# Attention on one Trainium2 core: an own order of two steps for the first half of the rows

## The chip, the cores and the metric

The kernel runs on one core of a Trainium2 chip. The metric is the device time of one execution in microseconds (us); lower is better. Before the change it is 2920.76 us, the median of three runs (2920.69 to 2922.99).

## What is computed

A transformer block for one sequence of 2048 rows and 576 columns, float32: a modulation drawn from a condition vector, layer norm, softmax attention with 32 heads of 18 columns, a second layer norm, and a gated product with 4608 hidden columns. The attention is what matters here:

```python
q, k, v = qkv[0], qkv[1], qkv[2]
scale = Dh ** -0.5
scores = jnp.einsum("bhqd,bhkd->bhqk", q, k) * scale
p = _softmax(scores, axis=-1)
o = jnp.einsum("bhqk,bhkd->bhqd", p, v)
```

## The kernel before

The attention is cut into 32 **units** `u`: units 0 to 15 are the first 1024 query rows, one unit for each pair of heads, and units 16 to 31 the other 1024 rows. A unit has 16 **steps** `kt`, one for each tile of 128 keys. Two steps in a row, an even and an odd one, are called a pair of steps here, so a unit has eight. TensorE's instructions run in the order in which the program writes them (lines 922 and 923 fix that); the order of the other engines is made by the framework's planner, from what is ready.

What a step issues is spelled by a string, one letter for each act (line 47: one string for even steps, one for odd steps):

- **t** (line 959): the transposed scores of 128 keys by 512 queries, one matmul of 56 rows. There are four in a step, for two chunks of queries and the two heads. The heads alternate, t0 and t2 take head 0, t1 and t3 head 1. Head 0 lies on partitions 0 to 63, head 1 on 64 to 127. ScalarE turns the result into `p` with an exponential (line 963).
- **m** (`turn`, line 490): one more piece of `maxima` (lines 426 to 469), which runs 64 pieces a unit, about one and a half units ahead: a score matmul of 54 rows (line 446), again with the heads alternating, of which VectorE takes the maximum of each row (line 459). From the third unit's maxima on, of every eight pieces the first goes to a relu on ScalarE (line 452), and the third is then taken by a VectorE operation (line 454) that adds the relu's result; the six others are plain maxima. In the first two units' maxima all eight are plain.
- **v** (`values`, line 528): the products of the oldest step's `p` with the values, four matmuls on four column strips of 32, which the trace shows as eight. A run of these is a **value run**. They add up in the one bank `o` over the 16 steps.
- **w** (lines 551 and 553): in odd steps, side work. `taken` (line 546) copies the finished `o` to `oT` on ScalarE, in the step kt = 1; `outputs` (line 554) transposes `oT` by four matmuls and scales it, at kt = 3; `spread` (line 471) transposes the maxima of the next unit, and its DMAs write them into the unit's `q` tile, at kt = 13. From unit 15 on, w also takes pieces of the projection behind the attention.

Every score matmul and every transpose takes the next of seven PSUM banks in turn (`bank`, line 78), so each waits until the work on the bank seven places before it is done. `p` has three buffers (line 520).

The two strings before are, with the acts numbered as above:

```python
STEPS = "vtmmttmvtm", "tmttwmtmm"
```

An even step holds two value runs, for the two steps before it, and an odd step none. Between the two runs lie t0, m, m, t1, t2, m; behind the second, t3, m, and then the odd step's t0, m, t1, t2, w, m, t3, m, m. `turns["to"]` caps how far `maxima` may be ahead; 89 pieces are done before the loop starts, and each step then does four.

Of the kernel before, what the change touches and what calls it, by code (L numbers as in the profile page):

```python
# [27 lines left out]
H = 32  # L28
DH = 18
VW = DH + 1  # L30
NT = S // P
# [7 lines left out]
LEAD = 6  # L39
# [4 lines left out]
NB = F // 256  # L44
LAG = 2

STEPS = "vtmmttmvtm", "tmttwmtmm"
ORDERED = 56


# [1 line left out]
def tile_block(ctx, tc, x_in, wqkv, wo, w_gate, w_up, w_down, c_in, w_mod, out):  # L52
# [20 lines left out]
    small = left.enter_context(tc.tile_pool(name="small", bufs=2))  # L73
    sc = early.tile([P, 5], F32, name="sc")

    turns = {"s": 0, "to": 65 + 4 * LEAD, "bank": 0}

    def bank():

        turns["bank"] += 1  # L80
        return ps.tile([P, 512], F32, name=f"s{turns['bank'] % 7}")


    def load_mod(a, b, i):

        cols = slice(2 * D * i, 2 * D * (i + 1))
        for t in range(0, 4, 2):
            rows = slice(t * P, (t + 2) * P)
            nc.sync.dma_start(a[:, t : t + 2, :], w_mod[rows, cols].rearrange("(t p) c -> p t c", p=P))
        nc.sync.dma_start(b[0:64, :], w_mod[DM:D, cols])  # L90
        return [a[:, t, :] for t in range(4)] + [b]
# [311 lines left out]
    def heads(u):  # L403
        return qsets[u % 3], ksets[u if u < 2 else 2 + (u - 2) % 3]

    def load_heads(u):


        qs, ks = heads(u)
        half, p = divmod(u, H // 2)  # L410
        own = slice(half * HW, (half + 1) * HW)
        for h in range(2):
            rows = slice((2 * p + h) * DH, (2 * p + h + 1) * DH)
            two, one = (slice(64 * h + a, 64 * h + b) for a, b in ((0, 2 * DH), (2 * DH, 3 * DH)))
            nc.sync.dma_start(
                qs[two, :].bitcast(F32), qd[:, rows, own].rearrange("l f n -> f l n").bitcast(F32)
            )
            nc.sync.dma_start(qs[one, :].bitcast(F32), qd[0, rows, own].bitcast(F32))
            wide = S if h or u < 2 else S + 512
            nc.sync.dma_start(  # L420
                ks[two, 0:wide].bitcast(F32),
                kd[0, rows, 0:wide].unsqueeze(1).to_broadcast([DH, 2, wide]).bitcast(F32),
            )
            nc.sync.dma_start(ks[one, 0:wide].bitcast(F32), kd[1, rows, 0:wide].bitcast(F32))
# [65 lines left out]
    def turn():  # L490
        if turns["s"] < turns["to"]:
            turns["s"] += 1
            next(todo, None)
# [52 lines left out]
    def taken():  # L546

        if "whole" in state:
            half, p, acc = state.pop("whole")
            oT = epool.tile([P, 512], F32, name="oT")  # L550
            nc.scalar.copy(oT, acc)  # L551
            state["end"] = (half, p, oT)

    def outputs():

        if "end" not in state:
            return
        half, p, oT = state.pop("end")
        tp = bank().rearrange("p (b q) -> p b q", q=P)
        for b in range(4):  # L560
            nc.tensor.transpose(tp[:, b, :], oT[:, b * P : (b + 1) * P], ident)  # L561

        tq = tp.rearrange("p b (j e) -> p j b e", e=32)
        rec = epool.tile([P, 4, 4], F32, name="rec")
        nc.vector.reciprocal(rec, tq[:, :, :, DH])
        if half == 1 and p == H // 2 - 1:
            state["last"] = epool.tile([P, 512], F32, name="oT")[:, 0 : 16 * DH].rearrange("p (t e) -> p t e", t=8)
            for h in range(2):
                nc.vector.tensor_tensor(
                    state["last"][:, :, h * DH : (h + 1) * DH].rearrange("p (c b) e -> p c b e", c=2),  # L570
                    tq[:, 2 * h : 2 * h + 2, :, 0:DH],
                    rec[:, 2 * h : 2 * h + 2, :].unsqueeze(3).to_broadcast([P, 2, 4, DH]),
                    op=ALU.mult,
                )
            return
        nc.scalar.copy(oT, tp.rearrange("p b q -> p (b q)"))
        tq = oT.rearrange("p (b j e) -> p j b e", j=4, e=32)
        for h in range(2):
            f0 = (2 * p + h) * DH
            nc.gpsimd.tensor_tensor(  # L580
                Os[half][:, :, f0 : f0 + DH].rearrange("p (c b) e -> p c b e", c=2),
                tq[:, 2 * h : 2 * h + 2, :, 0:DH],
                rec[:, 2 * h : 2 * h + 2, :].unsqueeze(3).to_broadcast([P, 2, 4, DH]),
                op=ALU.mult,
            )
# [341 lines left out]
    for u in range(UNITS):  # L927
        half, p = divmod(u, H // 2)
        qs, ks = heads(u)
        if 0 < u < UNITS - 2:  # L930
            load_heads(u + 2)
        if u == H // 2:
            Os.append(big.tile([P, 8, 640], F32, name="big"))
        for kt in range(NT):
            step = u * NT + kt
            turns["to"] = 65 + 4 * LEAD + 4 * (step + 1)
            kcols = slice(kt * P, (kt + 1) * P)
            probs = []
            for does in STEPS[kt % 2]:
                if does == "m":  # L940
                    turn()
                elif does == "w":
                    if kt == 3:
                        outputs()
                    taken()
                    if "spread" in state:
                        spread(*state.pop("spread"))
                    if FROM0 <= step < FROM1:
                        next(rows0, None)
                    if step >= FROM1:  # L950
                        next(rows1, None)
                elif does == "v":
                    if step >= LAG:
                        values()
                else:
                    c, h = divmod(len(probs), 2)
                    sT = bank()
                    rows = slice(64 * h, 64 * h + 3 * DH + 2)
                    nc.tensor.matmul(  # L959
                        sT, ks[rows, kcols], qs[rows, c * 512 : (c + 1) * 512], start=True, stop=True  # L960
                    )
                    pr = ppool.tile([P, 512], F32, name=f"p{len(probs)}")
                    state["exp"] = nc.scalar.activation(pr, sT, AF.Exp, scale=SCALE)  # L963
                    probs.append(pr)
            pending.append((half, p, kt, probs))
            if u in (1, 3):
                if kt == 2:
                    a = big.tile([P, 8, 640], F32, name="big")
                    a = a.rearrange("p a b -> p (a b)")[:, 0 : 8 * D].rearrange("p (t c) -> p t c", t=4)
                    b = slots.tile([P, 2560], F32, name="w0")[:, 0 : 2 * D]  # L970
                    mods = load_mod(a, b, 1 + u // 2)
                    row = slots.tile([P, 2560], F32, name="w1")[:, 0:544]
                elif kt == 10 and u == 1:
                    modulate(row, mods, HALVES, [(None, None), (mcol2[:, 1, :], 0.0)])
                elif kt == 10:
                    modulate(row, mods, HALVES, [(mcol2[:, 0, :], 1.0), (gb_b, None)])
            if 4 * NT <= step < FROM0 and step % 2 == 0:
                next(downs, None)
            if step == FROM0:
                for _ in downs:  # L980
                    pass
            if step == FROM1 - 1:
                for _ in rows0:
                    pass
                bgs.close()
                raws = ctx.enter_context(tc.tile_pool(name="raws", bufs=1, side="right"))
            if u == 30 and kt == 7:
                first = [load_block(raws, 0, k, paced) for k in range(2)]
            if u >= 30 and kt == 2:
                load_x(u - 30, f"k{u - 30}")  # L990
            if u == UNITS - 1 and kt == 3:
                nc.sync.dma_start(oend[:, :, 0 : D - DL - 2 * DH], Os[1][:, :, DL : D - 2 * DH])
            if u == UNITS - 1 and kt == 9:
                for _ in rows1:
                    pass
                load_x(2, "w0")
                load_x(3, "w1")
                both = big.tile([P, 2, 5, 512], F32R, name="big")
                for i in range(2):
                    X[5 + i] = both[:, i]  # L1000
                    load_x(5 + i)
                begun = {"b": 0, "half": 0, "raw": first}
                for k in ORDER[:2]:
                    weights_operand(begun, k, True)
# [196 lines left out]
    for n, (hf, b, k) in enumerate(seq):  # L1201
# [51 lines left out]
        if hf == 0 and b == NB - 1:  # L1253
            s = ORDER.index(k)
# [31 lines left out]
```

## Time and profile before

| | |
|---|---|
| median of three runs | 2920.76 us |
| the profiled execution | 2920.71 us |
| its span, first to last instruction | 2918.9 us |
| TensorE's granted clock over the span | 0.993 of full |
| busy share of PE / DVE / ACT / POOL | 98% / 73% / 55% / 28% |
| units 0 to 15 (237.5 to 896.9 us) | 659.4 us |
| units 16 to 31 (896.9 to 1588.8 us) | 691.9 us |
| the gated product (1588.8 us to the end) | 1330.1 us |

The profile's page gives busy time by engine; the windows give it by stage. A busy PE says little by itself: a matmul's record lasts longer than the interval at which the next one starts. So the stage is read by the start times of matmuls, from one value run to the next, and by what each of them waited for.

### The profile page before, as it was taken

How to read it: one execution, taken by the hardware profiler on the slowest of the kernel's cores; microseconds unless marked ns; L12 is line 12 of the kernel's file. 1: busy time of each engine (PE TensorE's matmuls, PEld its weight loads, DVE VectorE, ACT ScalarE, POOL GpSimd, SP SyncE). 2: the span in 40 equal slices, each digit the busy share in tenths (PEclk: the TensorE clock that was granted, in tenths of full speed). 3: DMA queues.
4: the chain of work that ended last, by engine and by line, in shares of the span. 5: the costliest groups of instructions: out<-in, count | busy, mean ns of one | idle time of the engine just before them, and what ended most of it. 6: DMA issues, size and time to landing. Idle time of an engine off the chain costs nothing.

```text
span 2918.9 us, 46640 instructions
## 1 busy us (share of the span) xinstructions
PE 2855.8 (98%) x17141; PEld 1880.8 (64%) x17141; DVE 2135.0 (73%) x3896; ACT 1614.4 (55%) x3022; POOL 814.1 (28%) x972
## 2 busy tenths in 40 slices
PE   7999999999999999999999999988999999999999
PEld 5874333343334443443443888877888888888888
DVE  7567888888888888998882777756777555555555
ACT  3227889999998888999888333333333111111111
POOL 3102014444213111661103544467543100000000
PEclk9999999999999999999999999999999999999999
DMA  5344123333212110221125866676666844444443
GB/s 176 115 147 145 49 76 131 122 125 123 90 49 77 34 53 21 99 95 63 50 86 185 289 220 234 232 250 237 225 211 238 300 167 169 167 168 167 159 159 137
DMA packets 137261, 425.97 MB, mean 146 GB/s; under 512 B 18884, under 2 KB 56520, under 8 KB 124744
## 3 DMA queue, kind: packets, MB, share of 16 engines
q1 hardware_dynamic: 121272, 342.42, 34.7%
q0 software_dynamic: 15760, 80.56, 7.8%
q8 instruction: 135, 2.21, 0.3%
q14 instruction: 94, 0.77, 0.1%
HBM read 264.45 MB, written 157.95 MB: 145 GB/s over the span
## 4 chain that ended last, share of the span: by engine, by line
PE 89%; DMA 3%; ACT 3%; DVE 2%; POOL 2%; issue 1%; SPq 1%; POOLq 0%; ACTq 0%; DVEq 0%
PE o L537 17%; PE x L1031 14%; PE d L1067 14%; PE s L959 13%; PE s L446 11%; PE bg L1031 5%; PE bu L1031 5%; PE s L294 3%; PE s L334 2%; PE s L676 2%; ACT p L963 2%; DMA xs<-ho 1%; DMA B<-hs 1%; PE s L561 1%; ACT oT L551 1%
## 5 line engine op out<-in xcount | busy, mean ns | idle before, releaser
L963 ACT ACTIVATE p<-s 128x512 f32<-128x512 f32 x2048 | 1068.5, 608 | 141.2 <-PE s L446 91.8
L459 DVE TENSOR_REDUCE mx<-s 128x1 f32<-128x512 f32 x1568 | 1015.4, 685 | 142.2 <-PE s L446 128.2
L446 PE MATMUL s<-k,q 54*128 54x512 f32 x1920 | 649.2, 439 | 2.1 <-ACT p L963 1.6
L959 PE MATMUL s<-q,k 56*128 56x512 f32 x1920 | 578.5, 433 | 2.7
L959 PEld LDWEIGHTS s<-q,k 56*128 56x128 f32 x1920 | 274.5, 185 | 472.2 <-ACT p L963 304.0
L537 PE MATMUL o<-p,vaug 128*32 128x512 f32 x4096 | 555.0, 607 | 0.0
L1067 PE MATMUL d<-wd,hh 128*128 128x288 f32 x2304 | 469.4, 298 | 20.9 <-DVE Oa L1071 20.7
L1067 PEld LDWEIGHTS d<-wd,hh 128*128 128x128 f32 x2304 | 379.0, 191 | 29.9 <-DVE Oa L1071 24.4
L1071 DVE TENSOR_TENSOR Oa<-Oa,d 128x288 f32<-128x288 f32 x576 | 257.8, 452 | 151.4 <-PE d L1067 147.8
L446 PEld LDWEIGHTS s<-k,q 54*128 54x128 f32 x1920 | 308.1, 185 | 69.2 <-ACT p L963 38.5
L1067 PE MATMUL d<-wd,hl 128*128 128x288 f32 x1152 | 343.7, 298 | 0.1
L1031 PE MATMUL x<-k,w 128*128 128x512 f32 x994 | 238.3, 390 | 0.5 <-DVE u L1245 0.5
L1043 ACT ACTIVATE u<-u 128x512 f32<-128x512 f32 x72 | 45.5, 632 | 328.9 <-DVE u L1233 310.3
L1067 PEld LDWEIGHTS d<-wd,hl 128*128 128x128 f32 x1152 | 219.7, 191 | 0.3 <-DVE hl L1047 0.3
L1031 PEld LDWEIGHTS x<-k,w 128*128 128x128 f32 x994 | 184.1, 188 | 37.5 <-DVE u L1245 0.9
L537 PEld LDWEIGHTS o<-p,vaug 128*32 128x32 f32 x4096 | 83.5, 108 | 164.7 <-issue 149.2
L1040 ACT ACTIVATE sg<-x 128x512 f32<-128x512 f32 x36 | 21.5, 598 | 285.1 <-PE x L1031 285.1
L1073 POOL DMA_DIRECT2D out_dram<-Oa x16 | 8.7, 544 | 606.4 <-DVE Oa L1071 606.4
L454 DVE CUSTOM_DVE_ANT_0 rise<-s,rise 128x512 f32<-128x512 f32 x240 | 163.4, 681 | 0.0
L452 ACT ACTIVATE rise<-s 128x512 f32<-128x512 f32 x240 | 151.4, 631 | 0.0
L918 POOL TENSOR_TENSOR w<-S,w 64x256 fp32r<-64x256 f32 x69 | 72.2, 1046 | 212.9 <-ACT w L913 202.4
L1031 PE MATMUL x<-w,w 128*128 128x512 f32 x504 | 123.5, 395 | 0.0
(240 smaller groups left out, 3772.7 us busy)
## 6 DMA issues: line engine op xcount, KB each, us to landing
w<-ws SPq DMA_DIRECT2D x126, 640.0 KB
ws<-w SPq DMA_DIRECT2D x124, 640.0 KB
wd<-wds SPq DMA_DIRECT2D x36, 1152.0 KB
wds<-w POOLq DMA_DIRECT2D x18, 1152.0 KB, 4.5
k<-kd SPq DMA_DIRECT2D x30, 360.0 KB
w<-in_B_w_down_dram POOLq DMA_DIRECT2D x18, 576.0 KB, 5.0
q<-qd SPq DMA_DIRECT2D x64, 144.0 KB
raw<-in_B_w_gate_dram SPq DMA_DIRECT2D x34, 256.0 KB
```

Source lines behind the costliest of these rows:

```text
L294: nc.tensor.matmul(acc, w, hT[:, t, cols], start=n == 0, stop=n == len(ts_) - 1)
L446: nc.tensor.matmul(sp, qs[rows, qt * P : (qt + 1) * P], ks[rows, kc * 512 : (kc + 1) * 512], start=True, stop=True,)
L452: nc.scalar.activation(rise, sp, AF.Relu)
L454: nc.vector.tensor_tensor_reduce(rise, sp, rise, 1.0, -3.0e38, ALU.add, ALU.max, mx[0][:, qt, 0:1])
L459: nc.vector.tensor_reduce(mx[h][:, qt, j : j + 1], sp, axis=AX.X, op=ALU.max)
L537: nc.tensor.matmul(acc[32 * j : 32 * j + 32, :], vaug[:, kt, (2 * p + h) * VW : (2 * p + h) * VW + 32], probs[2 * c + h], start=kt == 0, s ...
L918: eng.tensor_sub(w[rows, :, to, :], src[rows, :, a, :], w[rows, :, a, :].bitcast(F32))
L959: nc.tensor.matmul(sT, ks[rows, kcols], qs[rows, c * 512 : (c + 1) * 512], start=True, stop=True)
L963: state["exp"] = nc.scalar.activation(pr, sT, AF.Exp, scale=SCALE)
L1031: nc.tensor.matmul(acc[v], w[:, v, a, :], X[s][:, b, :], start=first and n == 0, stop=n == 6, skip_group_check=not first,)
L1067: nc.tensor.matmul(acc[:, :HALF], a[:, f, rows], w[:, f, cols], start=n == 0, stop=n == 5)
L1071: nc.vector.tensor_add(Oa[:, t, cols], Oa[:, t, cols], acc[:, :HALF])
```

## The change

The first half of the rows (units 0 to 15) gets strings of its own: one value run at the head of each step, for the step two before; w right behind the odd step's run; five pieces of `maxima` in the even step and three in the odd one. One piece less is done before the loop (88), and the last step of the first half does one more (`TURN`), so that unit 16 starts as before. From unit 16 on the old strings stand. The cap on `maxima` is set a little higher in the loop, so that five fit.

```diff
-STEPS = "vtmmttmvtm", "tmttwmtmm"
+EASY = "vmmtmmtttm", "vwmtmttmt"
+TURN = "vwmtmttmtm"
+FULL = "vtmmttmvtm", "tmttwmtmm"
...
-    turns = {"s": 0, "to": 65 + 4 * LEAD, "bank": 0}
+    turns = {"s": 0, "to": 64 + 4 * LEAD, "bank": 0}
...
-            turns["to"] = 65 + 4 * LEAD + 4 * (step + 1)
+            turns["to"] = 64 + 4 * LEAD + 4 * (step + 2)
...
-            for does in STEPS[kt % 2]:
+            order = (EASY if u < H // 2 else FULL)[kt % 2]
+            for does in TURN if step == NT * H // 2 - 1 else order:
```

## Rows read from the trace of the kernel before

**Rows 1.** The profile's page: the span, TensorE's granted clock in 40 slices.

```profile
span 2918.9 us, 46640 instructions
...
PEclk9999999999999999999999999999999999999999
```

**Rows 2.** Windows by stage: length, then busy time of each engine (instructions), clock.

```profile
core 0: us, PE busy (x) PEld busy (x) DVE busy (x) ACT busy (x) POOL busy (x), PEclk, DMA share, GB/s
237.50:896.90 659.40, 655.86 (x4247) 261.38 (x4247) 576.40 (x1096) 603.18 (x1195) 205.92 (x310) 0.99 0.29 97
896.90:1588.80 691.90, 688.87 (x4571) 300.35 (x4571) 566.69 (x1099) 606.41 (x1190) 199.71 (x276) 1.00 0.22 71
```

**Rows 3.** Timeline of PE, a plain pair of unit 10: start, length, what, count.

```profile
672.24 1.06 PE L537 MATMUL o<-p,vaug 128*32 128x512 f32 x8
673.23 0.50 PE L959 MATMUL s<-q,k 56*128 56x512 f32 x1
673.24 0.73 PE L446 MATMUL s<-k,q 54*128 54x512 f32 x2
673.58 0.62 PE L959 MATMUL s<-q,k 56*128 56x512 f32 x2
673.81 0.39 PE L446 MATMUL s<-k,q 54*128 54x512 f32 x1
674.13 1.06 PE L537 MATMUL o<-p,vaug 128*32 128x512 f32 x8
675.12 0.49 PE L959 MATMUL s<-q,k 56*128 56x512 f32 x1
675.13 0.72 PE L446 MATMUL s<-k,q 54*128 54x512 f32 x2
675.46 0.62 PE L959 MATMUL s<-q,k 56*128 56x512 f32 x3
675.92 0.40 PE L446 MATMUL s<-k,q 54*128 54x512 f32 x1
676.30 0.49 PE L959 MATMUL s<-q,k 56*128 56x512 f32 x1
676.64 0.65 PE L446 MATMUL s<-k,q 54*128 54x512 f32 x2
677.22 1.07 PE L537 MATMUL o<-p,vaug 128*32 128x512 f32 x8
```

**Rows 4.** Timeline of ACT in the same pair.

```profile
673.08 0.64 ACT L452 ACTIVATE rise<-s 128x512 f32<-128x512 f32 x1
673.83 1.58 ACT L963 ACTIVATE p<-s 128x512 f32<-128x512 f32 x3
675.65 2.07 ACT L963 ACTIVATE p<-s 128x512 f32<-128x512 f32 x4 [0.25 <-PE s L446]
```

**Rows 5.** Timeline of DVE in the same pair.

```profile
671.92 1.28 DVE L459 TENSOR_REDUCE mx<-s 128x1 f32<-128x512 f32 x2
673.80 0.69 DVE L459 TENSOR_REDUCE mx<-s 128x1 f32<-128x512 f32 x1 [0.60 <-PE s L446]
```

**Rows 6.** Waits within unit 10 (653 to 694 us): total, times, longest.

```profile
PEld s L959 <- ACT p L963: 9.9, 15, 0.8
PEld s L959 <- DVE mx L459: 5.9, 7, 0.8
```

**Rows 7.** Timeline of PE, unit 10: first value runs around kt 0 to 3, the transposes.

```profile
651.88 1.07 PE L537 MATMUL o<-p,vaug 128*32 128x512 f32 x8
...
657.02 1.06 PE L537 MATMUL o<-p,vaug 128*32 128x512 f32 x8
...
660.83 0.66 PE L561 MATMUL s<-ident,oT 128*128 128x128 f32 x4
661.41 0.50 PE L446 MATMUL s<-k,q 54*128 54x512 f32 x1
...
662.25 1.07 PE L537 MATMUL o<-p,vaug 128*32 128x512 f32 x8
```

**Rows 8.** Timeline of PE, unit 10: value runs and transpose around kt 12 to 15.

```profile
682.21 1.06 PE L537 MATMUL o<-p,vaug 128*32 128x512 f32 x8
...
686.01 0.28 PE L475 MATMUL s<-ident,nm 128*16 128x128 f32 x1
686.29 0.50 PE L446 MATMUL s<-k,q 54*128 54x512 f32 x1
...
687.44 1.07 PE L537 MATMUL o<-p,vaug 128*32 128x512 f32 x8
```

**Rows 9.** Timeline of ACT: the copy of `o` in unit 10.

```profile
654.97 0.59 ACT L551 COPY oT<-o 128x512 f32<-128x512 f32 x1
```

**Rows 10.** Timeline of PE: first value runs of two pairs of unit 0.

```profile
248.50 1.07 PE L537 MATMUL o<-p,vaug 128*32 128x512 f32 x8
...
253.55 1.06 PE L537 MATMUL o<-p,vaug 128*32 128x512 f32 x8
```

## The prediction

> **What bounds the kernel now.** I read the windows by stage first: the change touches only units 0 to 15, 659.4 us of the span, at full clock [rows 1, 2]. There PE is busy 655.9 us, ACT 603.2 and DVE 576.4, so the totals name nobody and the stage must be read by matmul starts. The timeline of one plain pair of unit 10 [rows 3] shows the period, from the first value run at 672.24 to the next at 677.22: 4.98 us. The reader should see five intervals in it. The first score matmuls start 0.99 behind the start of a run. The next ones start 0.35 later, then 0.23 for each further pair of two heads side by side. The run starts 0.32 behind the last (674.13 after 673.81). A lone matmul on an occupied half also takes 0.23 (the third t of the group at 675.46 starts at 675.69, as 0.62 less 0.39; the m follows at 675.92). And behind a matmul that had to wait, the next on the same half is 0.34 later (676.30 to 676.64), and the run 0.43 behind its start (the second of the two at 676.64 starts at 676.79; run at 677.22).
>
> Now the wait. t3, first behind the second run at 675.12, is exponentiated from 675.65 for 0.60 [rows 4], to 676.25; the odd step's t3 needs that bank and starts at 676.30. The last m of the pair needs the next exponential's bank, 0.49 later (four in 2.07, less 0.60, over three). Chain: 1.89 to the second run, 0.99, 1.13 until the exponential ends, 0.05, 0.49, 0.43 to the next run: 4.98, which is the period measured. So **the bound is a round trip over the second value run, ScalarE and the seven banks**, not an engine at its limit: ACT idles 0.25 and DVE 0.60 in the pair [rows 4, 5]. The waits of the unit say the same, most of them on the exponential [rows 6].
>
> **The change, part by part.** No work is added: each pair of steps keeps eight t, eight m and two runs. What moves is the order.
>
> *Row halves.* Eight pieces a pair keep the head's phase; with 88 done ahead, the even step starts with the relu's piece on head 0. By heads the even step reads m0 m1 | t0 | m0 m1 | t1 t2 | t3 m0, and the odd one m1 t0 | m0 t1 | t2 m1 | t3, where numbers behind m are heads and bars part what can run side by side. That is nine slots where the old order has eight: two lone matmuls more, one joined less. I charge 0.23 for the ninth. The row shows that order is kept: a lone m at 675.92 isn't passed by the t behind it [rows 3]. The Trainium skill says so as a rule (TensorE: Matmul & The Clock Gate, Part 3, what overlaps and what doesn't: matmuls start and end strictly in order). By that rule alone, were PE the bound, the change would lose 0.23 in each of 128 pairs, 29 us.
>
> *The walk of a plain pair*, run at 0, all intervals from [rows 3 to 5]: m, m at 1.00; t0 1.34; m, m 1.57; t1, t2 1.80. t3 is the eighth and takes the bank of the first m, whose relu ends 1.13 behind the matmul's start (the exponential's figure; a relu's record is no shorter [rows 4]), at 2.13: t3 at 2.18. The next m takes the second m's bank. A reduce ends 1.25 behind its matmul's start (673.24 to 673.80 plus 0.69 [rows 5]), at 2.25: m at 2.30, and the run at 2.30 + 0.43 = 2.73. Behind it 3.73, 4.07, 4.30, 4.53, and the next run at 4.85. I looked for waits in the second gap: the exponentials follow at 0.49 (2.13, 2.62, 3.11, 3.60, 4.09), so the bank that the odd step's t2 needs is free at 4.14, 0.16 ahead of it; the others have more. Result **4.85 against 4.98 to 4.99: 0.14 less**. Without the one wait left it would be 4.48; that is the lower bound.
>
> *The copy of `o`* (kt = 1). Before it adds 0.15 (651.88 to 657.02 is 5.14 [rows 7]). Now it stands right behind the run that it needs. It is ready at 2.73 + 1.06 + 0.04 = 3.83, but the exponentials before it end at 4.09, so it ends at 4.58 and pushes the odd step's by 0.08 to 0.2; the relu of the next pair is late by 0.04. Pair 4.89, 0.24 less. It is also an **added wait**: the next step starts with a run that overwrites `o`, at 4.89, with 0.26 to spare, where before the copy ended at 655.56 and the run started at 657.02 [rows 7, 9]. Behind that run PE's whole queue would stand, and ACT and DVE behind it.
>
> *The four transposes* (kt = 3). They hold PE for 0.58 (660.83 to 661.41 [rows 7]). Before, the stalled gap hid most: the pair is 5.23, 0.24 over a plain one. Now that gap is full, so I charge all of it: 4.85 + 0.58 = 5.43, **0.20 more**. If the other wait hid them all, it would be 0.38 less; I see nothing that does. Right behind a run they need one change of array shape less than between scores. The Trainium skill has that as a rule (TensorEngine Tiling (Array Packing), Key Properties: switching the tiling mode drains TensorE), and the 0.35 and 0.32 on either side of a run against 0.23 agree. *The transpose of the maxima* (kt = 13) costs 0.28 (686.01 to 686.29 [rows 8]): 5.13 against 5.23, 0.10 less. Its copy and DMAs start no later against the next unit than before.
>
> *A unit*: 5 x -0.14 - 0.24 + 0.20 - 0.10 = -0.84 us. Fifteen units: -12.6.
>
> *Unit 0* computes plain maxima of unit 1 in its first five pairs, with no relu. Both first pieces are then DVE's: 2.25 and 2.85, m at 2.90, run at 3.33, pair 5.45 against 5.05 [rows 10]. That is +0.40 for three pairs, for five at most (the first two have another shape, with hardly a run); less 0.4 for its last three. I take +1.2. `TURN`'s extra m runs beside t3 and costs nothing, the 0.23 of a slot at most. Units 16 to 31 start from the same bank order and count of pieces and keep their 691.9 us [rows 2]; I allow 1 us either way, a choice. POOL's and SP's work is the same and mostly idle time's: POOL is busy 206 of 659 us [rows 2].
>
> **Sum**: -12.6 + 1.2 = -11.4. The profiled execution took 2920.71 us, 0.05 from the median: forecast **2909.3 us**.
>
> **Rivals.**
> *The copy and the side work eat it.* If the planner sets the copy of `o` behind one or two of the odd step's exponentials, the run waits until 5.1 or 5.6 instead of 4.89: 0.2 to 0.7 in each of 15 units, 3 to 11 us: 2913 to 2920. For it: only 0.26 spare. Against: the copy comes first in the program.
> *The first consumers come late: slower.* Everything hangs on the first two banks of the even gap. The relu may slip from 2.13 to 2.25 at no cost; at some 2.34 the gain is gone. If ScalarE takes it behind t0's exponential (ends 2.37), it ends at 2.86, t3 starts at 2.91, the run at 3.34, the pair is 5.46: +0.61 in 120 pairs, 73 us, 2982. In between, each 0.1 is 12 us. For it: the order of ScalarE is not fixed by the program. Against: the relu's matmul starts 0.34 before t0's.
> *The last wait is not paid.* If banks come back sooner than their rows say, the pair tends to 4.48, 44 us less: 2865; half way, 2887. Against: both round trips are read from many equal pairs.
>
> **How the numbers follow.** Forecast, 2903 to 2914.5: 0.55. Side work, no measurable change: 0.20. Late consumers: 0.16. Wait not paid, below 2903: 0.09. About 0.2% (5.8 us) is what a measurement of this kernel tells from no change, so faster 0.64, same 0.20, slower 0.16. The range leaves out the far end of the last two, some 0.06 below and 0.12 above: 2896 to 2928. The forecast's own range is 2903 to 2914.5.
>
> **What would show it.** Right: plain pairs of units 2 to 15 at 4.85 with the second run at 2.73; a wait of t3 on the relu and of the m on the reduce, and no wait in the odd gap; the transposes' pair at 5.43; unit 0's early pairs at about 5.45; units 16 to 31 unchanged. Wrong: a plain pair over 4.95; a run that waits for the copy of `o`; a relu that ACT starts behind an exponential of its own step; or second-half units that change.

## The result, and the profile after

The changed kernel takes 2929.85 us, the median of seven runs (2926.83 to 2932.73), against 2920.69 us before (seven runs, 2916.49 to 2924.56). The ratio is 1.0033, with a 95% interval of 1.0021 to 1.0045: **slower by a third of a per cent**, where 2909.3 us was forecast, with a range of 2896 to 2928.

Periods are given in this table by the start of each step's first exponential, so that they don't depend on where a run stands in the step (two pairs that the prediction read by runs as 5.23 are 5.19 and 5.18 here); units 4 to 14 agree to some 0.05 us in most pairs, and unit 9 is typical.

| us | before | forecast | after |
|---|---|---|---|
| a plain pair of steps | 5.00 | 4.85 | 4.86 |
| pair kt 0, 1 (copy of `o`) | 5.14 | 4.89 | 4.87 |
| pair kt 2, 3 (four transposes) | 5.19 | 5.43 | **5.90** |
| pair kt 12, 13 (transpose of the maxima) | 5.18 | 5.13 | **5.84** |
| the unit | 40.58 | 39.74 | 40.93 |
| unit 0 | 43.1 | 44.3 | 45.9 |
| start of the first exponential | 237.5 | 237.5 | 240.1 |
| units 1 to 15 together | 616.3 | 603.7 | 621.5 |

The stage after is read as before. First PE in a plain pair of unit 10 (start, length, what, count), to be laid beside [rows 3]:

```profile
678.18 1.07 PE L539 MATMUL o<-p,vaug 128*32 128x512 f32 x8
679.18 0.50 PE L448 MATMUL s<-k,q 54*128 54x512 f32 x1
...
680.31 1.07 PE L539 MATMUL o<-p,vaug 128*32 128x512 f32 x8
681.31 0.73 PE L448 MATMUL s<-k,q 54*128 54x512 f32 x3
681.65 0.62 PE L962 MATMUL s<-q,k 56*128 56x512 f32 x2
681.88 0.39 PE L448 MATMUL s<-k,q 54*128 54x512 f32 x1
682.12 0.87 PE L962 MATMUL s<-q,k 56*128 56x512 f32 x2
682.63 0.50 PE L448 MATMUL s<-k,q 54*128 54x512 f32 x1
683.06 1.07 PE L539 MATMUL o<-p,vaug 128*32 128x512 f32 x8
```

The odd step's gap, behind the run at 678.18, lasts 2.13 from run to run and the even one's 2.75; the walk gave 2.12 and 2.73. In the even gap the first two pieces, which start at 681.31, are read by ScalarE's relu and by a maximum of VectorE, and t3 and the last m wait for these two, as walked:

```profile
681.85 0.60 ACT L454 ACTIVATE rise<-s 128x512 f32<-128x512 f32 x1
681.88 0.69 DVE L461 TENSOR_REDUCE mx<-s 128x1 f32<-128x512 f32 x1 [0.28 <-PE s L448]
```

The relu ends 2.14 behind the run's start (forecast 2.13) and the maximum 2.26 (2.25). Over units 1 to 15 the t's wait on the relu comes in 120 pairs, which is all of them:

```profile
PEld s L962 <- ACT rise L454: 45.6, 120, 0.4
```

Now the same engine around the four transposes, at kt = 3, in place of [rows 7]:

```profile
667.42 1.07 PE L539 MATMUL o<-p,vaug 128*32 128x512 f32 x8
668.42 0.66 PE L563 MATMUL s<-ident,oT 128*128 128x128 f32 x4
669.00 0.49 PE L448 MATMUL s<-k,q 54*128 54x512 f32 x1
669.01 0.73 PE L962 MATMUL s<-q,k 56*128 56x512 f32 x2
669.34 0.64 PE L448 MATMUL s<-k,q 54*128 54x512 f32 x2
669.58 0.40 PE L962 MATMUL s<-q,k 56*128 56x512 f32 x1
670.16 0.49 PE L962 MATMUL s<-q,k 56*128 56x512 f32 x1 [0.18 <-ACT oT L578]
670.59 1.07 PE L539 MATMUL o<-p,vaug 128*32 128x512 f32 x8
```

The transposes hold PE for 0.58 as forecast (668.42 to 669.00). But the last t of the step, at 670.16, comes 0.58 behind the pair before it instead of 0.23, and what it waited for is named: the copy to `oT` (L578). Seven banks back from that t stands the transposes' own bank, since behind w the odd step has exactly seven score matmuls. ACT and DVE in the same stretch show what held that bank:

```profile
669.53 0.58 ACT L578 COPY oT<-s 128x512 f32<-128x512 f32 x1 [0.72 <-DVE rec L567]
670.01 1.58 ACT L966 ACTIVATE p<-s 128x512 f32<-128x512 f32 x3
```

```profile
669.18 0.26 DVE L567 RECIPROCAL rec<-s 128x16 f32<-128x16 f32 x1 [0.40 <-PE s L563]
```

The reciprocal ends at 669.44, the copy runs from 669.53 to 670.11, and the t starts 0.05 later. At kt = 13, in place of [rows 8], PE and then DVE:

```profile
693.78 0.28 PE L477 MATMUL s<-ident,nm 128*16 128x128 f32 x1
...
695.45 0.50 PE L962 MATMUL s<-q,k 56*128 56x512 f32 x1 [0.50 <-DVE mrows L480]
695.88 1.07 PE L539 MATMUL o<-p,vaug 128*32 128x512 f32 x8
```

```profile
694.52 0.69 DVE L461 TENSOR_REDUCE mx<-s 128x1 f32<-128x512 f32 x1 [0.42 <-PE s L962]
695.13 0.27 DVE L480 TENSOR_TENSOR mrows<-s,mrows 16x128 fp32r<-16x128 f32 x1
```

The subtraction that reads the bank last (L480) stands in DVE's queue behind a maximum of the odd step itself (694.52), so it ends at 695.40 and the t starts at 695.45. Over units 1 to 15 the list of waits of the changed kernel has both, fifteen times each:

```profile
PEld s L962 <- DVE mrows L480: 14.0, 15, 0.9
...
PEld s L962 <- ACT oT L578: 9.4, 15, 0.6
```

In the list of before, the subtraction does not occur. The same copy (L576 there) does, before the weight load of the first t behind the next run:

```profile
PEld s L959 <- ACT oT L576: 12.6, 15, 0.8
```

That one cost nothing. In unit 10 the copy is over at 663.00, and the t starts at 663.25, 1.00 behind the start of the run at 662.25 [rows 7], as first matmuls behind a run do:

```profile
662.38 0.61 ACT L576 COPY oT<-s 128x512 f32<-128x512 f32 x1
```

### The profile page after: what moved, and what is told of

Its sections match the earlier page's. It is cut to its first block, busy times and chain, and to the rows that moved or that the text cites. A ratio compares the mean times of both kernels' runs of the same rounds, so it can differ in the third digit from the quotient of the medians.

```text
span 2929.8 us, 46673 instructions
## 1 busy us (share of the span) xinstructions
PE 2857.6 (98%) x17141; PEld 1892.1 (65%) x17141; DVE 2132.2 (73%) x3896; ACT 1612.9 (55%) x3022; POOL 813.6 (28%) x972
## 4 chain that ended last, share of the span: by engine, by line
PE 89%; POOL 3%; DVE 2%; DMA 2%; ACT 2%; issue 2%; SPq 1%; POOLq 0%; DVEq 0%; ACTq 0%
PE o L539 17%; PE d L1070 14%; PE x L1034 14%; PE s L962 12%; PE s L448 11%; PE bg L1034 5%; PE bu L1034 5%; PE s L296 3%; PE s L336 2%; PE s L678 2%; PE s L563 1%; ACT p L966 1%; POOL S L881 1%; POOL z L771 0%; DMA wm<-in_w_mod_dram 0%
## 5 line engine op out<-in xcount | busy, mean ns | idle before, releaser
L448 PE MATMUL s<-k,q 54*128 54x512 f32 x1920 | 609.9, 444 | 2.1 <-ACT p L966 1.6
L962 PE MATMUL s<-q,k 56*128 56x512 f32 x1920 | 598.5, 430 | 10.4 <-DVE mrows L480 6.9
L962 PEld LDWEIGHTS s<-q,k 56*128 56x128 f32 x1920 | 302.4, 186 | 320.1 <-ACT p L966 169.2
L448 PEld LDWEIGHTS s<-k,q 54*128 54x128 f32 x1920 | 289.0, 185 | 222.5 <-ACT p L966 91.4
```

Source lines behind the costliest of these rows:

```text
L448: nc.tensor.matmul(sp, qs[rows, qt * P : (qt + 1) * P], ks[rows, kc * 512 : (kc + 1) * 512], start=True, stop=True,)
L962: nc.tensor.matmul(sT, ks[rows, kcols], qs[rows, c * 512 : (c + 1) * 512], start=True, stop=True)
```

## The experiments

The theory now (S): the transposes' own bank comes due at the odd step's last t, and its readers are late. Its rivals: the transposes cost a second because the array changes shape next to a run (D), or the copies that ScalarE takes between exponentials cost it (Q). The times in the expectations are by the start of exponentials or of runs, which differ by a few hundredths.

**The transposes ahead of the run.** `outputs` and `spread` get a letter of their own, x, ahead of the odd step's v; the copy of `o` stays behind it.

```diff
-EASY = "vmmtmmtttm", "vwmtmttmt"
-TURN = "vwmtmttmtm"
+EASY = "vmmtmmtttm", "xvwmtmttmt"
+TURN = "xvwmtmttmtm"
...
+                elif does == "x":
+                    if kt == 3:
+                        outputs()
+                    if "spread" in state:
+                        spread(*state.pop("spread"))
                 elif does == "w":
                     if kt == 3:
                         outputs()
...
```

The branch of w stays as it was: in the first half it finds this work done, and in the second half, whose strings have no x, it does it.

> The changed kernel with outputs and spread moved ahead of the odd step's value run (the copy of o stays behind it). Theory S (the seventh bank): the odd gap holds exactly seven score matmuls, so t3, the last, takes the bank of the transpose at its head and waits until that bank has been read; ahead of the run the reading is hidden by it. Then the pair of kt 2 and 3 falls from 5.91 to about 5.43 us, that of kt 12 and 13 from 5.83 to about 5.13, a unit from 40.9 to 39.8, the kernel by some 17 us, to about 2913. Rival D (the transposes cost a second in the array next to a run, by the changes of its shape): the shape changes as often as before, both pairs stay at 5.8 to 5.9 and the time at 2930. Rival Q (the copies that ScalarE puts between the exponentials delay the gap): they stay in its queue, both pairs within 0.1 of 5.9 and 5.8.

Measured: 2908.7 us, ratio to before 0.9955 (0.9941 to 0.9968). The pairs are 5.45 and 5.05 to 5.09 us, a unit 39.7. PE in unit 9:

```profile
610.53 0.66 PE L563 MATMUL s<-ident,oT 128*128 128x128 f32 x4
611.12 1.07 PE L539 MATMUL o<-p,vaug 128*32 128x512 f32 x8
612.11 0.50 PE L448 MATMUL s<-k,q 54*128 54x512 f32 x1
...
612.69 0.63 PE L967 MATMUL s<-q,k 56*128 56x512 f32 x2
613.25 1.07 PE L539 MATMUL o<-p,vaug 128*32 128x512 f32 x8
```

The transposes hold 0.59 and the gap behind the run is 2.13 again, as in a plain pair: the run hides the reading. The same transposes, the same copies and as many changes of shape cost 1.2 us less a unit. D falls. The copies have moved within ScalarE's queue together with the transposes, so for Q the next two versions, which leave them behind the run, count more. This version beats both kernels. Its units 1 to 15 take 603.3 us, where 603.7 was forecast for the change: once the wait is hidden, the sum of the prediction comes out.

**The bank read by ScalarE's copy alone.** w stays where the change has it.

```diff
-        nc.vector.reciprocal(rec, tq[:, :, :, DH])
...
         nc.scalar.copy(oT, tp.rearrange("p b q -> p (b q)"))
         tq = oT.rearrange("p (b j e) -> p j b e", j=4, e=32)
+        nc.vector.reciprocal(rec, tq[:, :, :, DH])
...
-        nc.scalar.copy(parts[0], tp)
-        nc.vector.tensor_sub(parts[1], tp, parts[0].bitcast(F32))
+        raw = parts[1].bitcast(F32)
+        nc.scalar.copy(raw, tp)
+        nc.gpsimd.tensor_copy(parts[0], raw)
+        nc.gpsimd.tensor_sub(parts[1], raw, parts[0].bitcast(F32))
```

> The changed kernel, w where it is, but the bank of the transposes is read by ScalarE's copy alone: the reciprocal is taken from the copy in SBUF, and the maxima are split by POOL from a copy in SBUF. Theory S: the copy can start right behind the transposes and ends before the odd step's t3 comes up (1.2 against 1.3 us in the gap), the bank of the maxima is free at 0.85: no wait, pairs at about 5.43 and 5.13 us, some 17 us less. Rival D: pairs unchanged at 5.9 and 5.8, time unchanged. Rival Q: the copies are in ScalarE's queue as before, pairs within 0.15 of what they are.

Measured: 2954.5 us, ratio 1.0109 (1.0086 to 1.0132). The two pairs are 5.54 and 5.06 us (S: 5.43 and 5.13), a quiet unit 39.8; but units 5, 16, 24 and 31 start 3 to 11 us late. Waits of SP and of PE around the start of unit 16:

```profile
SPq L486 <- POOL mrows L482: 43.2, 1, 43.2
```

```profile
PE s L965 <- DMA q<-mrows: 9.9, 1, 9.9
```

The split of the maxima now stood behind POOL's other work, and the DMAs that write them into `q` with it. The edit brought a cost of its own, so the total tells nothing; the next one takes POOL out.

**The same, split by ScalarE and VectorE.** From ScalarE's copy in SBUF:

```diff
-        nc.gpsimd.tensor_copy(parts[0], raw)
-        nc.gpsimd.tensor_sub(parts[1], raw, parts[0].bitcast(F32))
+        nc.scalar.copy(parts[0], raw)
+        nc.vector.tensor_sub(parts[1], raw, parts[0].bitcast(F32))
```

> As e2_sbuf, but the split of the maxima is ScalarE's and VectorE's, from ScalarE's copy in SBUF, so that it doesn't queue behind POOL's other work. Theory S: pairs at about 5.54 and 5.06 as in e2_sbuf, and no late unit starts (the first pairs of units 5, 15 and 16 at 4.86 to 5.2 instead of 7.8 to 15): unit 39.8, total some 15 us under the changed kernel, about 2913. If the late starts came from something other than POOL's queue they stay, and the total is 2930 or more.

Measured: 2922.85 us, ratio to before 0.9995 (0.9985 to 1.0005). Up to unit 16 it is as S has it: pairs of 5.55 and 5.06 us, most units 39.8, units 1 to 15 together 605.0 us against 621.5 of the changed kernel. PE and ACT in unit 9:

```profile
612.56 0.66 PE L565 MATMUL s<-ident,oT 128*128 128x128 f32 x4
...
613.72 0.72 PE L965 MATMUL s<-q,k 56*128 56x512 f32 x2
614.37 1.06 PE L541 MATMUL o<-p,vaug 128*32 128x512 f32 x8
```

```profile
613.30 0.59 ACT L580 COPY oT<-s 128x512 f32<-128x512 f32 x1 [0.36 <-PE s L565]
```

The transposes stand behind the run as in the changed kernel, and the pair is 0.35 shorter: the copy starts at 613.30, 0.74 behind the start of the transposes instead of 1.11, and the t starts 0.05 behind its end. In the other pair ScalarE has one copy more than in the changed kernel, and it is 0.78 shorter. That settles S against D and Q at the place itself. The total was missed: of the gain, 12 us are lost behind unit 16, 7 of them in unit 23 (48.7 us, before 41.6), whose last pair takes 12.05. `spread` is shared by both halves, and SP's queue waited there for its DMAs (6.4 us for DVE). Why the planner puts that work late I didn't follow up.

**The control: the same edit in the order before** (with POOL's split).

> The kernel before, with the bank of the transposes read by ScalarE's copy alone, as a control. Theory S: in the old order the seventh bank behind w comes up only past the next value run, so nothing waits for it: units stay at 40.57 us, pairs at 5.23 within 0.05. If VectorE's share of the work was itself what cost, they would be shorter by 0.2 or more.

Measured: one run, 2968.5 us, with late unit starts as in the version with POOL's split (unit 15: 49.6 us). Its pairs are the old ones: 5.20 and 5.18, plain 5.00, a quiet unit 40.58. In the old order, taking VectorE off that bank gains nothing.

**w ahead of the odd step's last t.**

```diff
-EASY = "vmmtmmtttm", "vwmtmttmt"
-TURN = "vwmtmttmtm"
+EASY = "vmmtmmtttm", "vmtmttmwt"
+TURN = "vmtmttmwtm"
```

> The changed kernel with w moved to just ahead of the odd step's last t (vmtmttmwt). Theory S: the bank of the transposes then comes due seven matmuls later, in the even gap behind the next run, long after it has been read, so no wait; the transposes stand between score matmuls and cost PE 0.58 us and two changes of shape: the pair of kt 2 and 3 about 5.64, that of kt 12 and 13 about 5.33, a unit about 40.2. Rival D (changes of the array's shape are what costs): one change more than behind the run, so both pairs at 5.9 and 5.8 or more.

Measured: one run, 2916.47 us. Pairs 5.65 and 5.44, units 40.25. PE in unit 9:

```profile
615.78 0.39 PE L962 MATMUL s<-q,k 56*128 56x512 f32 x1
616.10 0.66 PE L563 MATMUL s<-ident,oT 128*128 128x128 f32 x4
616.68 0.49 PE L962 MATMUL s<-q,k 56*128 56x512 f32 x1
617.11 1.07 PE L539 MATMUL o<-p,vaug 128*32 128x512 f32 x8
```

With transposes between score matmuls the step has one change of shape more, and still the pairs are 0.2 to 0.4 shorter than right behind the run. Against the version ahead of the run they are 0.20 and 0.37 longer. The 0.20 I put down to the change of shape, which the prediction had right in kind: the transposes start 0.32 behind the t before them, where a score matmul would start 0.23 behind it, and the run 0.43 behind the t that follows, where it is 0.32 in a plain odd step. The 0.37 is not that alone, and the pair is 0.11 over what was expected. The transpose of the maxima takes a bank in the middle of the gap, so the step's last t gets that of the gap's first piece, whose maximum ends at 641.50. The weight load of this t waits for it:

```profile
641.56 0.18 PEld L962 LDWEIGHTS s<-q,k 56*128 56x128 f32 x1 [0.28 <-DVE mx L461]
```

**The old order in unit 0.**

```diff
-    turns = {"s": 0, "to": 64 + 4 * LEAD, "bank": 0}
+    turns = {"s": 0, "to": 65 + 4 * LEAD, "bank": 0}
...
-            order = (EASY if u < H // 2 else FULL)[kt % 2]
+            order = (EASY if 0 < u < H // 2 else FULL)[kt % 2]
+            if step == NT - 1:
+                order = "tmttwmtm"
```

> The changed kernel with the old order in unit 0 (89 pieces ahead, one fewer in unit 0's last step, the new order from unit 1). If the plain maxima of unit 0's first five pairs cost the new order its place there, unit 0 goes from 45.9 back to 43.1 us and the kernel loses 2.8 us of 2930; units 1 to 15 stay at 40.9. If unit 0's extra time came from the start of the kernel and not from the order, it stays above 45.

Measured: unit 0 takes 43.3 us and units 1 to 15 stay at 40.9, as expected. But not all of the 2.7 us less are the plain maxima's. Its third to fifth pairs are 1.2 shorter together, that of kt 12 and 13 0.65, and the other two behind them 0.5 longer. The remaining 1.3 lie in the first two pairs (12.6 against 13.9 us), where executions differ in TensorE's clock: in the three profiles in which it stays at full (w ahead of the last t, the split by ScalarE and VectorE, and the next version), the new strings take 10.0 there. The total is 2929.6 us, ratio 1.0023 (1.0010 to 1.0037), which doesn't part from the changed kernel's interval: 2.8 us less is not shown in the time.

**The new strings in units 21 to 26 as well**, with the transposes and the pieces of the projection ahead of the run.

```diff
-            order = (EASY if u < H // 2 else FULL)[kt % 2]
-            for does in TURN if step == NT * H // 2 - 1 else order:
+            easy = u < H // 2 or 21 <= u < 27
+            order = (EASY if easy else FULL)[kt % 2]
+            if step == 21 * NT - 1:
+                order = "tmttwmtm"
+            for does in TURN if step in (NT * H // 2 - 1, 27 * NT - 1) else order:
...
+                    if u >= 21 and FROM0 <= step < FROM1:
+                        next(rows0, None)
...
-                    if FROM0 <= step < FROM1:
+                    if FROM0 <= step < FROM1 and not 21 <= u < 27:
                         next(rows0, None)
```

> As e1_ahead, and the same strings in units 21 to 26, with the pieces of the projection ahead of the run as well. If the round trip of the old order is the bound there too, their plain pairs go from 4.99 to 4.86, each unit is 0.8 us shorter, 5 us in all, about 2904. If these units are bound by the side pieces, they stay at 40.6 to 41.6.

Measured: 2906.49 us, ratio 0.9946 (0.9928 to 0.9963), not to be told from the version without it (0.9955). Plain pairs there do go to 4.86, but pairs with a side piece are 5.45 to 5.9 where they were 5.2 to 5.5, and the six units together take 245.5 us where they took 246.5: neither of the two outcomes expected.

## Why the prediction was wrong

**Right: the walk.** The plain pair was forecast at 4.85 and is 4.86, with gaps of 2.13 and 2.75 against 2.12 and 2.73. The number of slots (four ahead of t3 in the even gap, three in the odd one) and the wait on the first two banks of the even gap come out of [rows 3 to 5] at the size given. What stands beside what in that gap does not: t0 was to stand alone, but a piece starts with it (681.65, the third of the group at 681.31) and another with t1 (681.88), and t2 is alone (682.12). By the walk's order of heads the piece behind t0 is on the same half, so either a later piece started ahead of it or the halves do not bind as assumed; the records don't say which. The row at 675.92, read as showing that order is kept, does not test it: the t behind that m waited until 676.25 for its bank. The time is not touched, since t2 starts 1.81 behind the run, walked at 1.80. The pair with the copy of `o` was forecast at 4.89 and is 4.87. In unit 10 the copy ends at 664.39 and the run that overwrites `o` starts at 664.68, so it doesn't wait:

```profile
663.75 0.64 ACT L553 COPY oT<-o 128x512 f32<-128x512 f32 x1
```

```profile
664.68 1.07 PE L539 MATMUL o<-p,vaug 128*32 128x512 f32 x8
```

The plain maxima of unit 0 cost what was said: its third and fourth pairs take 5.42, forecast 5.45, before 5.05.

**Wrong: the part "the four transposes", and with it that of the maxima.** The step that failed is "now that gap is full, so I charge all of it: 4.85 + 0.58", and "costs 0.28: 5.13". I counted what the transposes take of PE, and looked for waits in the odd gap only for the plain pair. But a transpose also takes a bank, and the gap goes on with seven score matmuls, so the last of them gets that bank again. The terms measured 5.90 and 5.84: 0.47 and 0.71 more than forecast. Over fifteen units that is 17.7 us, and the forecast of -12.6 for them became +5.2 (621.5 against 616.3).

The first wait could have been worked out from the code and the trace of before. The code has the readers, the reciprocal and then the copy, and the trace has their times:

```profile
661.69 0.25 DVE L565 RECIPROCAL rec<-s 128x16 f32<-128x16 f32 x1
```

This starts 0.86 behind the transposes (660.83 [rows 7]). With 0.25 for it, 0.61 for the copy and 0.05, the t starts at 1.77, where without a wait it would start at 1.39; measured, 1.74. The run then starts 0.43 behind it instead of 0.32, which makes 0.49 in all (measured 0.47). The second could only have been seen as a risk: where VectorE's queue takes the subtraction is the planner's choice, and a maximum ahead of it takes 0.69 [rows 5].

**The rest of the sum.** Unit 0 is 1.7 us over its forecast: its pair of kt 12 and 13 (5.84) is the same miss, and its first two pairs, left out of the walk, took 0.4 and 0.9 longer, at half clock for longer (last section). The first exponential starts 2.7 us later in this execution. It starts between 236.9 and 241.5 us over the nine profiles of this case (241.5 in the old order), so I take that for a difference of executions and not the change's. Together: -11.4 forecast, +17.8 for units 1 to 15, +1.7, +2.7, and 0.1 in all that follows, make 10.9; the two profiled executions differ by 10.86. Some 4 us of this, the late start and the first two pairs of unit 0, are thus not shown to be the change's.

**The rivals.** "The copy and the side work eat it" had the right place, w, and the wrong wait: not the run behind the copy of `o`, but the score matmul behind the transposes' bank; its price of 3 to 11 us was too low. "The first consumers come late" didn't happen; the relu and the maximum end as walked. "The last wait is not paid" didn't either.

## What to carry to other kernels

Where buffers go round in a fixed turn, an instruction that is moved brings its buffer with it: count which later instruction gets that buffer, and who must have read it by then, on whichever queue its readers stand. A side piece belongs where something long that needs no buffer of the pool lies between it and that instruction; in the first half here, a value run (in units 21 to 26, with the projection's pieces, it gained nothing that the time shows). When a steady loop has been walked through, the pairs with side work need a walk of their own; here they were two pairs of eight, and they turned the sign.

## What the runs showed of the hardware

How long TensorE runs at half its clock where the attention begins differs between executions. PE waits there for the first operands: between 236 and 240 us it is busy 3.11 of 4 us in the changed kernel, and 3.00 in the last of the executions below. Windows of the kernel before, the changed kernel, and the version with units 21 to 26, in this order:

```profile
244.00:248.00 4.00, 4.00 (x19) 1.43 (x17) 2.45 (x5) 2.14 (x6) 3.89 (x3) 0.65 0.98 376
248.00:252.00 4.00, 4.00 (x31) 1.47 (x29) 3.98 (x8) 3.08 (x8) 3.89 (x3) 1.00 0.63 203
```

```profile
244.00:248.00 4.00, 4.00 (x17) 1.73 (x9) 2.04 (x5) 1.64 (x5) 3.27 (x2) 0.50 0.92 304
248.00:252.00 4.00, 4.00 (x16) 1.36 (x15) 2.32 (x4) 1.64 (x5) 3.89 (x3) 0.50 0.91 349
```

```profile
244.00:248.00 4.00, 3.89 (x27) 1.32 (x28) 3.79 (x7) 2.92 (x7) 3.89 (x3) 1.00 0.98 365
248.00:252.00 4.00, 3.81 (x24) 1.71 (x24) 3.76 (x8) 2.70 (x6) 3.94 (x2) 1.00 0.75 264
```

The third number from the right is the granted clock: 0.50 is 1.2 GHz, 1.00 is 2.4. In the changed kernel's execution it stays at half through both windows and in the last execution it is at full there, though both run the same strings in unit 0 but for the transposes. The first two pairs of unit 0 take 13.9 us in the one and 10.0 in the other. Why the clock falls in the one and not in the other stays open.
